# Crossbar transposes of queries and keys issued two steps ahead, in a fused ReLU-squared attention and channel-mixer kernel

## The chip, the cores and the metric

The kernel runs on one core of one Trainium2 chip. The metric is the device time of one execution in microseconds, lower is better; the profile gives the span from the first to the last instruction, which is 1.7 to 1.8 us shorter than the timed run. Every run is of one core, and a run counts as fast where it lies within 1.5% of the fastest of the same kernel in its series. "Landing" is the moment at which a transfer has arrived; the "granted clock" is the share of TensorE's full clock that the records show, and 0.5 is called half clock. In the profile lines PE is TensorE, PEld its weight loads, DVE the vector engine, ACT ScalarE, POOL GpSimd and SPq the queue of SyncE.

## The reference, cut to what matters

```python
# q, k, v: (8 batches, 12 heads, 448 tokens, 64), float32
scores = matmul(q, k.transpose(0, 1, 3, 2)) / sqrt(64)
attn   = maximum(scores, 0) ** 2 / 448
x      = heads side by side of matmul(attn, v)                      # (8, 448, 768)
u      = x + (maximum(x.T @ w_tok1, 0) @ w_tok2).T                  # token mixing, 448 -> 256 -> 448
out    = u + maximum(u @ w_ch1, 0) @ w_ch2                          # channel mixing, 768 -> 1536 -> 768
```

Scores need queries and keys with the head dimension on partitions, but they arrive with tokens on partitions. So every group of four heads needs one transpose of q and k. There are 24 groups, called steps 0 to 23 here.

## The kernel before

Steps 0 to 10 are transposed by TensorE, steps 11 to 23 by a DMA transpose (through the crossbar) on the SyncE queue, out of a staging buffer `qk_sb` into which the vector engine interleaves q and k. The parts that the change and the argument touch:

```python
    TDMA = 11
    def interleave(i):                      # vector engine, L192
        t = attn.tile([128, 2, QC, 2, D], BF16, name="qk_sb", bufs=1)
        qk_tiles[i] = t
        for w in range(2):
            nc.vector.tensor_copy(t[:, w].rearrange("n c g d -> n g c d"), raws.pop((i, "qk"[w])))

    def transposes_dma(i):                  # SyncE queue, L198
        sb = attn.tile([128, 2, QC, 128], BF16, tag="qkT", name="qkT_x")     # pool attn: bufs=2
        nc.sync.dma_start_transpose(out=sb..., in_=qk_tiles.pop(i)...)
        qkT[i] = sb
    # ... cut: scores (L217 on TensorE, L231 on ScalarE, squares L238 on the vector engine),
    # ... values (L250), x_back (L294: a DMA transpose of x), u_back (L413: of u), token and channel layers

    for i in range(DB + 1, ND + 2):         # one step; DB = 3, ND = 24
        # ... cut
        if i < ND:
            scores(i, 0); scores(i, 1)
        if 0 <= i - 1 < ND:
            values(i - 1, range(QC)); values_out(i - 1)
        if i < ND:
            scores(i, 2)
        # ... cut: filler matmuls of the channel layers while i - 1 < XDMA
        if 0 <= i - 1 < ND:
            x_back(i - 1)
        # ... cut
            while u_later and ...:
                u_back(u_later.pop(0))
        if TDMA <= i + 1 < ND:
            transposes_dma(i + 1)           # for the next step
        if i + PRE < ND:                    # PRE = 3
            if i - 1 >= XDMA:
                nc.gpsimd.tensor_copy(gate, x_tiles[i - 1][:1, 1, 3, 127:])   # wait until x has landed
            load_four(i + PRE)              # six loads of q, k, v on the GpSimd queue
        square()
        # ... cut: filler matmuls; scores 3 and 4; transposes(i + 1) on TensorE while i + 1 < TDMA
        square()
        # ... cut: filler matmuls, token layer 1 (L339, L355), scores 5 and 6
        if not slow:
            square()
            fill(0.1, least=1)
        if back:
            token2(i - 1)                   # L380 on TensorE, L390 on the vector engine
        # ... cut
        square()
        if TDMA <= i + 2 < ND:
            interleave(i + 2)
        fill(1 / 3 if slow else 0.16, least=1)
```

`fill` takes ready-made units of channel work from a queue: six L431 matmuls (evacuated by ScalarE) or twelve L470 matmuls (evacuated by the vector engine, L477). The program fixes the order of the matmuls; a change of the waits leaves that order as it is.

Of the kernel before, what the change touches and what calls it, by code (L numbers as in the profile page):

```python
# [10 lines left out]
BF16 = mybir.dt.bfloat16  # L11
# [5 lines left out]
def kernel(  # L17
# [13 lines left out]
    B, H, S, D = q.shape  # L31
# [5 lines left out]
    ND = B * H // 4  # L37
    DB = H // 4
    QC = S // 64
# [12 lines left out]
    attn = ctx.enter_context(tc.tile_pool(name="attn", bufs=2))  # L52
# [70 lines left out]
    qkT, at2, squares, accs = {}, {}, [], {}  # L123

    def transposes(i, place="acc", split=False):
        sb = attn.tile([128, 2, 2, S], BF16, name="qkT")
        if place == "att":
            both = ps_att.tile([128, 2, 1024], BF16, tag="att", name="qkT_ps")
            parts = [both[:, r] for r in range(2)]
        else:  # L130
            pool, tags = (ps_acc, ("acc0", "acc1")) if place == "acc" else (ps_mm, ("bank", "bank"))
            parts = [pool.tile([128, 1024], BF16, tag=tag, name="qkT_ps1") for tag in tags]
        for w in (1, 0) if i == 0 else (0, 1):
            src = raws.pop((i, "qk"[w]))
            for c in range(QC):
                at = w * S + c * 64
                for r in range(2):
                    h = slice(64 * r, 64 * (r + 1))
                    for g in range(2):
                        nc.tensor.matmul(  # L140
                            parts[r][64 * g : 64 * (g + 1), at : at + 64],
                            lhsT=src[h, g, c, :],
                            rhs=ident[h, h],
                            is_transpose=True,
                            start=True,
                            stop=True,
                            skip_group_check=True,
                        )
        qkT[i] = sb
        if place == "att":  # L150
            nc.vector.tensor_copy(sb.rearrange("n r w t -> n r (w t)"), both[:, :, : 2 * S])
            return
        for r in range(2):
            (nc.scalar.copy if split and r == 0 else nc.vector.tensor_copy)(
                sb[:, r].rearrange("n w t -> n (w t)"), parts[r][:, : 2 * S]
            )

    def transposes_first():

        sb = attn.tile([128, 2, 2, S], BF16, name="qkT")  # L160
        qkT[0] = sb
        keys = [ps_acc.tile([128, 1024], BF16, tag=f"acc{r}", name="kT_ps") for r in range(2)]
        queries = ps_att.tile([128, 2, 1024], BF16, tag="att", name="qT_ps")
        for w, dst in ((1, keys), (0, [queries[:, r] for r in range(2)])):
            for c in range(QC):
                for r in range(2):
                    h = slice(64 * r, 64 * (r + 1))
                    for g in range(2):
                        nc.tensor.matmul(
                            dst[r][64 * g : 64 * (g + 1), c * 64 : c * 64 + 64],  # L170
                            lhsT=raws[0, "qk"[w]][h, g, c, :],
                            rhs=ident[h, h],
                            is_transpose=True,
                            start=True,
                            stop=True,
                            skip_group_check=True,
                        )
            if w:
                nc.scalar.copy(sb[:, 0, 1], keys[0][:, :S])
                nc.vector.tensor_copy(sb[:, 1, 1], keys[1][:, :S])  # L180
            else:
                nc.vector.tensor_copy(sb[:, :, 0], queries[:, :, :S])

    TDMA = 11
    qk_tiles = {}

    def interleave(i):
# [4 lines that stand above are left out]
            nc.vector.tensor_copy(  # L192
                t[:, w].rearrange("n c g d -> n g c d"), raws.pop((i, "qk"[w]))
            )

    def transposes_dma(i):
        sb = attn.tile([128, 2, QC, 128], BF16, tag="qkT", name="qkT_x")
        nc.sync.dma_start_transpose(  # L198
            out=sb.rearrange("n w c t -> n (w c) t"),
            in_=qk_tiles.pop(i).rearrange("n w c g d -> n (w c g d)"),  # L200
        )
        qkT[i] = sb

    def qk_of(i, h, r):
        sb = qkT[i]
        if i < TDMA:
            return sb[h, r, 0, :], [sb[h, r, 1, c * 64 : (c + 1) * 64] for c in range(QC)]
        cols = slice(64 * r, 64 * (r + 1))
        return sb[h, 0, :, cols], [sb[h, 1, c, cols] for c in range(QC)]

    def scores(i, c, alone=False):
        ps = ps_att.tile([128, 2, 512], FP32, tag="att", name="sc_ps")
        for r in range(2):
            for g in range(2):
                h = slice(64 * g, 64 * (g + 1))
                queries, keys = qk_of(i, h, r)
                nc.tensor.matmul(  # L217
                    ps[64 * r : 64 * (r + 1), g, :S],
                    lhsT=keys[c],
                    rhs=queries,  # L220
                    start=True,
                    stop=True,
                    skip_group_check=True,
                )
        at = attn.tile([128, 2, S], BF16, name="at", bufs=12)
        if alone:
            nc.vector.tensor_scalar(
                out=at, in0=ps[:, :, :S], scalar1=0.0, scalar2=None, op0=ALU.max
            )
        else:  # L230
            nc.scalar.activation(at, ps[:, :, :S], AF.Relu)  # L231
        squares.append(at)
        at2[i, c] = at
# [184 lines left out]
    def hold_back(b, src):  # L418

        u_tiles[b] = mix.tile([128, NP, NT - NT // 2, 128], BF16, name="u_sb", bufs=3)  # L420
        for p in range(NP):
            nc.gpsimd.tensor_copy(u_tiles[b][:1, p, 0, :1], src)
# [206 lines left out]
    i = DB  # L629
# [31 lines left out]
    for i in range(DB + 1, ND + 2):  # L661
        slow = i <= 2 * DB
        back = i - 1 < ND
        if i == 2 * DB + 1:
            rate[0] = (EC * C1 + NT * C2) / DB
        if i < ND:
            scores(i, 0)
            scores(i, 1)
        if 0 <= i - 1 < ND:
            values(i - 1, range(QC))  # L670
            values_out(i - 1)
        if i < ND:
            scores(i, 2)
        if i - 1 < XDMA:
            fill(1 / 3, least=1)
        if 0 <= i - 1 < ND:
            x_back(i - 1)
        since[0] = 0.0
        if i > 2 * DB + 1:
            if i == 2 * DB + 2:  # L680
                hold_back(1, x_tiles[i - 1][:1, 0, 0, :1])
            while u_later and u_later[0] < max(i - 1 - (i == 2 * DB + 2), 0):
                u_back(u_later.pop(0))
        if TDMA <= i + 1 < ND:
            transposes_dma(i + 1)
        if i + PRE < ND:
            if i - 1 >= XDMA:
                nc.gpsimd.tensor_copy(gate, x_tiles[i - 1][:1, 1, 3, 127:])  # L688
            load_four(i + PRE)
        if i == 5:  # L690
            load_wc2(1, 2)
            load_wt1_last()
        square()
        if i - 1 >= XDMA:
            fill(0.37, least=1)
        if i < ND:
            scores(i, 3)
            scores(i, 4)
        if i + 1 < min(ND, TDMA):
            transposes(i + 1)  # L700
        square()
        if slow:
            token1(i - 1)
            fill(1 / 3, least=1)
        else:
            fill(0.37, least=1, upto=4400 if back else 0)
            if back:
                token1_main(i - 1)
        if i < ND:
            if not slow:  # L710
                token1_rest(i - 1)
            scores(i, 5)
            scores(i, 6)
        elif back:
            token1_rest(i - 1)
# [4 lines that stand above are left out]
            token2(i - 1)  # L720
            if (i - 1) % DB == DB - 1:
                channel_work((i - 1) // DB)
        if i == 2 * DB + 1:
            hold_back(0, uT_tiles[1][:1, 0, :1])
            for _ in range(DB):
                u_back(u_later.pop(0))
        square()
        if TDMA <= i + 2 < ND:
            interleave(i + 2)
        fill(1 / 3 if slow else 0.16, least=1)  # L730
    while queue:
        queue.pop(0)[1]()
# [30 lines left out]
```

## Time and profile before

| | before |
|---|---|
| time, median of the runs beside the changed kernel | 385.73 us (384.25 to 388.74, 4 runs; 387.2 of the first three was known to the prediction) |
| span of the profiled run | 385.1 us |
| TensorE busy, idle | 360.8 us, 24.3 us |
| TensorE waits for the crossbar transpose (L217 on qkT_x) | 15.4 us in 6 waits |
| granted TensorE clock, mean | 0.991 |

The page, the waits and a step are read line by line in the prediction below. It says that six loads are issued beside the transpose, but not what sets them off. That stands in the timeline of the kernel before, in the step that starts at 144.60 us:

```profile
151.44 0.18 POOL L688 COPY gate<-x_sb 1x1 bf16<-1x1 bf16 x1 [7.44 <-DMA x_sb<-xT]
...
151.95 1.19 POOL L83 DMA_DIRECT2D q_raw<-in_q_dram  x2 [0.34 <-issue]
```

Columns of the timeline: start, duration, engine, line, operation, tiles, then the idle time before it and what ended it. The loads wait behind a gate until x has landed; they start at 151.95 us, and the transpose of q and k is issued at 151.97 us (its line is in the prediction). The two set out together.

### The profile page before, as it was taken

Reading aid. Unit: us, or ns where it says so; the run is one execution under the profiler, and the core shown is the slowest. Engines: PE = TensorE matmul, PEld = TensorE weight load, DVE = VectorE, ACT = ScalarE, POOL = GpSimd, SP = SyncE. Lnnn points to the kernel's source line nnn. Section 1 sums busy time; section 2 is a strip of 40 time slices with the busy share of each in tenths; the row PEclk is TensorE's granted clock in tenths of the full one; section 3 lists DMA queues with packets and bytes.
Section 4 is the critical chain, followed back from the end, with each engine's and each line's share of the span. In section 5 each row is a group of like instructions: output and inputs, shape, how many; then the busy total and the mean of one; then the engine's idle time right before and its main releaser. Section 6 shows DMA issues by size and latency. Waiting matters only on the chain.

```text
span 385.1 us, 8830 instructions
## 1 busy us (share of the span) xinstructions
PE 360.8 (94%) x3649; PEld 193.2 (50%) x3649; DVE 208.4 (54%) x414; ACT 210.9 (55%) x313; POOL 99.0 (26%) x185
## 2 busy tenths in 40 slices
PE   8889999999999989899899999699949999999995
PEld 4444555556565544454455544355425555555564
DVE  2986788746567655656637655365523845321022
ACT  4987888764544577446664566534727437311400
POOL 9948346305030332131241232230300000000000
PEclk9999999999999999999999999989989999999999
DMA  8999999925998985896795987968755364234024
GB/s 154 123 203 171 194 195 159 142 36 92 186 113 171 234 156 88 143 174 147 121 138 119 204 137 135 118 81 202 115 69 97 78 142 97 54 44 107 0 51 115
DMA packets 93273, 49.19 MB, mean 128 GB/s; under 512 B 67185, under 2 KB 89777, under 8 KB 93233
## 3 DMA queue, kind: packets, MB, share of 16 engines
q0 software_dynamic: 24496, 21.49, 39.6%
q1 hardware_dynamic: 68352, 26.72, 34.6%
q8 instruction: 28, 0.46, 0.5%
q10 hardware_dynamic: 384, 0.43, 0.4%
q14 instruction: 13, 0.10, 0.1%
HBM read 43.42 MB, written 11.01 MB: 141 GB/s over the span
## 4 chain that ended last, share of the span: by engine, by line
PE 80%; DMA 12%; DVE 4%; ACT 1%; issue 1%; POOL 1%; ACTq 0%; DVEq 0%
PE m_ps L470 29%; PE m_ps L431 24%; DMA qkT_x<-qk_sb 11%; PE acc_ps L250 8%; PE sc_ps L217 8%; PE h_ps L380 3%; PE t_ps L339 2%; PE t_ps L321 1%; DVE uT_sb L390 1%; DVE at L238 1%; DMA k_raw<-in_k_dram 1%; PE warm_ps L566 1%; ACT at L231 1%; PE qkT_ps L140 1%; PE t_ps L355 1%
## 5 line engine op out<-in xcount | busy, mean ns | idle before, releaser
L231 ACT ACTIVATE at<-sc_ps 128x896 bf16<-128x896 f32 x167 | 144.9, 923 | 65.3 <-PE sc_ps L217 65.3
L238 DVE TENSOR_TENSOR at<-at 128x896 bf16<-128x896 bf16 x168 | 98.7, 620 | 65.8 <-ACT at L231 65.4
L431 PE MATMUL m_ps<-uT_sb,wc 128*128 128x448 bf16 x564 | 115.5, 353 | 0.2 <-DVE uT_sb L390 0.2
L470 PE MATMUL m_ps<-wc,r_sb 128*128 128x384 bf16 x660 | 114.0, 328 | 0.0
L470 PEld LDWEIGHTS <-r_sb 128*128 128x128 bf16 x660 | 63.0, 98 | 49.1 <-issue 9.1
L438 ACT ACTIVATE r_sb<-m_ps 128x448 bf16<-128x448 f32 x94 | 51.5, 548 | 53.0 <-PE m_ps L431 53.0
L431 PEld LDWEIGHTS <-wc 128*128 128x128 bf16 x564 | 52.3, 98 | 55.9 <-issue 11.1
L477 DVE TENSOR_TENSOR out_sb<-m_ps,u_sb 128x384 f32<-128x384 f32 x55 | 30.5, 554 | 45.3 <-PE m_ps L470 45.3
L250 PE MATMUL acc_ps<-at,v_raw 64*64 64x448 bf16 x672 | 40.5, 362 | 1.6 <-DVE x_sb L312 0.8
L217 PE MATMUL sc_ps<-qkT_x 64*64 64x448 bf16 x364 | 27.3, 363 | 15.4 <-DMA qkT_x<-qk_sb 15.4
L268 DVE TENSOR_SCALAR xT<-acc_ps 128x448 bf16<-128x448 f32 x45 | 26.1, 619 | 27.6 <-PE acc_ps L250 27.6
L688 POOL COPY gate<-x_sb 1x1 bf16<-1x1 bf16 x12 | 3.0, 248 | 131.3 <-DMA x_sb<-xT 131.3
L83 POOL DMA_DIRECT2D q_raw<-in_q_dram x48 | 28.9, 614 | 22.6 <-DMA wc<-in_moe_w_ch_dram 19.7
L390 DVE TENSOR_TENSOR uT_sb<-h_ps,xT 128x448 bf16<-128x448 f32 x48 | 27.7, 615 | 9.4 <-PE h_ps L380 9.3
L83 POOL DMA_DIRECT2D v_raw<-in_v_dram x48 | 29.6, 642 | 7.3 <-DMA wc<-in_moe_w_ch_dram 5.3
L250 PEld LDWEIGHTS <-v_raw 64*64 64x64 bf16 x672 | 21.1, 110 | 15.6 <-issue 5.0
L83 POOL DMA_DIRECT2D k_raw<-in_k_dram x46 | 28.2, 633 | 1.7 <-issue 1.7
L365 ACT ACTIVATE r_sb<-t_ps 128x256 bf16<-128x256 f32 x36 | 11.8, 381 | 30.1 <-PE t_ps L355 26.4
L217 PE MATMUL sc_ps<-qkT 64*64 64x448 bf16 x308 | 25.5, 360 | 0.9 <-ACT at L231 0.8
L380 PE MATMUL h_ps<-wt,r_sb 128*128 128x448 bf16 x96 | 22.3, 353 | 0.0
L217 PEld LDWEIGHTS <-qkT_x 64*64 64x64 bf16 x364 | 8.3, 107 | 25.8 <-DMA qkT_x<-qk_sb 18.3
L339 PE MATMUL t_ps<-x_sb,wt 128*128 128x256 bf16 x108 | 14.7, 273 | 0.0
(62 smaller groups left out, 161.4 us busy)
## 6 DMA issues: line engine op xcount, KB each, us to landing
out_dram<-out_sb SPq DMA_DIRECT2D x54, 192.0 KB, 3.3
q_raw<-in_q_dram POOLq DMA_DIRECT2D x48, 112.0 KB, 4.3
v_raw<-in_v_dram POOLq DMA_DIRECT2D x48, 112.0 KB, 6.8
k_raw<-in_k_dram POOLq DMA_DIRECT2D x46, 112.0 KB, 5.9
wc<-in_moe_w_ch_dram POOLq DMA_DIRECT2D x4, 1152.0 KB, 12.2
u_sb<-uT_sb SPq DMA_TRANSPOSE x48, 2.6
x_sb<-xT SPq DMA_TRANSPOSE x16, 3.3
k_first<-in_k_dram SPq DMA_DIRECT2D x1, 224.0 KB, 3.4
```

The costliest lines, as they stand in the source:

```text
L83: eng.dma_start(out=dst[64 * r : 64 * (r + 1)].rearrange("p g c d -> p g (c d)"), in_=src[b, h0 : h0 + 2].rearrange("g (p c) d -> p g (c d ...
L217: nc.tensor.matmul(ps[64 * r : 64 * (r + 1), g, :S], lhsT=keys[c], rhs=queries, start=True, stop=True, skip_group_check=True,)
L231: nc.scalar.activation(at, ps[:, :, :S], AF.Relu)
L238: nc.vector.tensor_tensor(out=at, in0=at, in1=at, op=ALU.mult)
L250: nc.tensor.matmul(ps[r][64 * g : 64 * (g + 1), :S], lhsT=v_raw[h, g, c, :], rhs=at[h, g, :], start=(c == 0), stop=(c == QC - 1), skip_gro ...
L268: nc.vector.tensor_scalar(out=xT[b % 2][:, 2 * d + r, :S], in0=ps[r][:, :S], scalar1=float(alpha2), scalar2=None, op0=ALU.mult,)
L380: nc.tensor.matmul(parts[r][:, :S], lhsT=r1[:, j, r * 128 : (r + 1) * 128], rhs=wt2[:, j, :], start=(j == 0), stop=(j == JC - 1),)
L390: nc.vector.tensor_tensor(out=uT_tiles[b // 2][:, 2 * d + r, off : off + S].rearrange("n (c p) -> n c p", c=QC), in0=parts[r][:, :S].rearr ...
L431: nc.tensor.matmul(ps[:, :S], lhsT=wc1[:, g, e * 128 : (e + 1) * 128], rhs=uT[:, g, off : off + S], start=(g == 0), stop=(g == CC - 1),)
L438: nc.scalar.activation(r2[:, e, off : off + S], ps[:, :S], AF.Relu)
L470: nc.tensor.matmul(ps[:, :HN], lhsT=r2[:, e, t * 128 : (t + 1) * 128], rhs=wc2[:, e, cols], start=(e == 0), stop=(e == EC - 1),)
L477: nc.vector.tensor_tensor(out=o[:, cols].rearrange("n (g d) -> n g d", d=128), in0=ps[:, :HN].rearrange("n (g d) -> n g d", d=128), in1=u_ ...
```

## The change

The intent is to take the crossbar transpose off TensorE's path by issuing it a step earlier. It needs its staged input earlier, so the interleaving copies move to the front of the step; a third transposed buffer is taken and one of twelve score buffers given up; and step 11 goes back to TensorE. The whole diff:

```diff
--- before.py
+++ after.py
@@ -123,7 +123,7 @@
     qkT, at2, squares, accs = {}, {}, [], {}
 
     def transposes(i, place="acc", split=False):
-        sb = attn.tile([128, 2, 2, S], BF16, name="qkT")
+        sb = attn.tile([128, 2, 2, S], BF16, name="qkT", bufs=3)
         if place == "att":
             both = ps_att.tile([128, 2, 1024], BF16, tag="att", name="qkT_ps")
             parts = [both[:, r] for r in range(2)]
@@ -157,7 +157,7 @@
 
     def transposes_first():
 
-        sb = attn.tile([128, 2, 2, S], BF16, name="qkT")
+        sb = attn.tile([128, 2, 2, S], BF16, name="qkT", bufs=3)
         qkT[0] = sb
         keys = [ps_acc.tile([128, 1024], BF16, tag=f"acc{r}", name="kT_ps") for r in range(2)]
         queries = ps_att.tile([128, 2, 1024], BF16, tag="att", name="qT_ps")
@@ -181,7 +181,7 @@
             else:
                 nc.vector.tensor_copy(sb[:, :, 0], queries[:, :, :S])
 
-    TDMA = 11
+    TDMA = 12
     qk_tiles = {}
 
     def interleave(i):
@@ -194,7 +194,7 @@
             )
 
     def transposes_dma(i):
-        sb = attn.tile([128, 2, QC, 128], BF16, tag="qkT", name="qkT_x")
+        sb = attn.tile([128, 2, QC, 128], BF16, tag="qkT", name="qkT_x", bufs=3)
         nc.sync.dma_start_transpose(
             out=sb.rearrange("n w c t -> n (w c) t"),
             in_=qk_tiles.pop(i).rearrange("n w c g d -> n (w c g d)"),
@@ -222,7 +222,7 @@
                     stop=True,
                     skip_group_check=True,
                 )
-        at = attn.tile([128, 2, S], BF16, name="at", bufs=12)
+        at = attn.tile([128, 2, S], BF16, name="at", bufs=11)
         if alone:
             nc.vector.tensor_scalar(
                 out=at, in0=ps[:, :, :S], scalar1=0.0, scalar2=None, op0=ALU.max
@@ -671,6 +671,8 @@
             values_out(i - 1)
         if i < ND:
             scores(i, 2)
+        if TDMA <= i + 2 < ND:
+            interleave(i + 2)
         if i - 1 < XDMA:
             fill(1 / 3, least=1)
         if 0 <= i - 1 < ND:
@@ -681,8 +683,8 @@
                 hold_back(1, x_tiles[i - 1][:1, 0, 0, :1])
             while u_later and u_later[0] < max(i - 1 - (i == 2 * DB + 2), 0):
                 u_back(u_later.pop(0))
-        if TDMA <= i + 1 < ND:
-            transposes_dma(i + 1)
+        if TDMA <= i + 2 < ND:
+            transposes_dma(i + 2)
         if i + PRE < ND:
             if i - 1 >= XDMA:
                 nc.gpsimd.tensor_copy(gate, x_tiles[i - 1][:1, 1, 3, 127:])
@@ -725,8 +727,6 @@
             for _ in range(DB):
                 u_back(u_later.pop(0))
         square()
-        if TDMA <= i + 2 < ND:
-            interleave(i + 2)
         fill(1 / 3 if slow else 0.16, least=1)
     while queue:
         queue.pop(0)[1]()
```

## The prediction

> **What bounds the kernel now.** I read the page's busy line and chain first, then the table of waits, then the timeline of single steps.
>
> ```profile
> PE 360.8 (94%) x3649; PEld 193.2 (50%) x3649; DVE 208.4 (54%) x414; ACT 210.9 (55%) x313; POOL 99.0 (26%) x185
> ...
> PE 80%; DMA 12%; DVE 4%; ACT 1%; issue 1%; POOL 1%; ACTq 0%; DVEq 0%
> PE m_ps L470 29%; PE m_ps L431 24%; DMA qkT_x<-qk_sb 11%; PE acc_ps L250 8%; PE sc_ps L217 8%; PE h_ps L380 3%; PE t_ps L339 2%; PE t_ps L321 1%; DVE uT_sb L390 1%; DVE at L238 1%; DMA k_raw<-in_k_dram 1%; PE warm_ps L566 1%; ACT at L231 1%; PE qkT_ps L140 1%; PE t_ps L355 1%
> ```
>
> TensorE sets the end: 94% busy, 80% of the chain. The one foreign piece of weight is the crossbar transpose of queries and keys (qkT_x), 11%, about 42 us. But the chain follows a released wait back to the transfer's issue, and TensorE was working through most of that time. What it lost is in the table of waits (us in total, times, longest):
>
> ```profile
> PEld L217 <- DMA qkT_x<-qk_sb: 18.3, 7, 6.3
> ...
> PE sc_ps L217 <- DMA qkT_x<-qk_sb: 15.4, 6, 5.8
> ...
> DVE qk_sb L192 <- DMA qkT_x<-qk_sb: 8.4, 2, 5.3
> DVE qk_sb L192 <- DMA k_raw<-in_k_dram: 4.1, 5, 1.2
> ```
>
> So 15.4 us in six waits is the prize; of the 24 us in which TensorE is idle at all (385.1 less 360.8), that is most. The six waits, read one by one before the first score matmul of a step, are 1.37, 1.44, 1.73, 1.42, 3.60 and 5.81 us. The timeline of one step shows why:
>
> ```profile
> 148.01 1.23 SPq L294 DMA_TRANSPOSE x_sb<-xT  x1
> 149.29 2.58 SPq L413 DMA_TRANSPOSE u_sb<-uT_sb  x2
> ...
> 151.97 1.59 SPq L198 DMA_TRANSPOSE qkT_x<-qk_sb  x1
> ...
> 157.77 0.57 PE L217 MATMUL sc_ps<-qkT_x 64*64 64x448 bf16 x8 [1.44 <-DMA qkT_x<-qk_sb]
> 157.85 0.39 DVE L192 COPY qk_sb<-q_raw 128x896 bf16<-128x896 bf16 x1 [0.92 <-DMA k_raw<-in_k_dram]
> ```
>
> The step starts at 144.60. The transpose for the next step stands third in the SyncE queue and is issued 7.4 us into it; it lands at 157.73. TensorE's own work in the step is done at 156.33 and it waits 1.44 us. The six waits stand at the ends of exactly the six steps whose TensorE work is only 11.7 to 12.9 us; steps of 14.6 us and more hide the transfer. The vector copy in the last line is charged to a key load, but those keys came a step earlier; it can start only when the transpose has read the single staging buffer qk_sb, so it too waits for this transfer.
>
> A long wait costs a second time:
>
> ```profile
> 273.98 10.16 DMA qkT_x<-qk_sb
> 284.19 0.96 PE sc_ps L217 x8
> 285.15 2.33 PE acc_ps L250 x27
> ...
> 301.73 1.32 PE acc_ps L250 x28
> ```
>
> After the 5.81 us wait, eight score matmuls take 0.96 us in place of 0.57 (0.57 stands in the other steps) and 27 value matmuls 2.33 us where 28 take 1.32. The clock records hold a stretch of 3.4 us at 0.5 there and another after the 3.60 us wait, where values take 1.99 and 24 output matmuls 4.79 in place of 4.01. Together 0.39 + 1.01 + 0.67 + 0.78 = 2.9 us.
>
> **What the Trainium skill says.** "TensorE: Matmul & The Clock Gate", Part 1: an idle window of about 3.4 us drops the array to half clock until about 3.4 us of work have passed. The trace agrees: both halved stretches are 3.41 us long and only the two waits above 3.4 us have one. "Trainium Kernel Development and Optimization", Key Constraints: DMAs from the SyncE, ScalarE and GpSimd queues share the same 16 DMA engines and interleave. The trace agrees: the transpose lands 4.6 and 5.5 us after issue in the last two steps, where no inputs are loaded, and 5.3 to 10.2 us where six loads are issued beside it. "Perfetto Trace Analysis", Tensor Engine Instruction: the vector engine is strictly first in, first out, so a copy that waits for data holds up all vector work behind it; the trace shows it, with vector idle up to 5.3 us ahead of L192.
>
> **The change, part by part.** I call step i the turn of the main loop that computes the scores of i.
>
> The transpose used in step i+2 is now issued in step i, at the same place of the SyncE queue, some 7.4 us in. Its deadline is a whole step later: 4 to 5 us of room (11.7 - 7.4) become 16 or more. The worst landing on record is 10.16 us. All six waits go: -15.4 us. The two halved stretches go with them: -2.9 us.
>
> Step 11 is transposed on TensorE once more. The same work in the step before shows its price:
>
> ```profile
> 106.26 0.39 PE L140 MATMUL qkT_ps<-ident,q_raw 64*64 64x64 bf16 x28
> 106.47 0.43 PE L140 MATMUL qkT_ps<-ident,k_raw 64*64 64x64 bf16 x28
> 106.84 4.07 PE L470 MATMUL m_ps<-wc,r_sb 128*128 128x384 bf16 x24
> ```
>
> 56 transposes take 106.84 - 106.26 = 0.6 us of TensorE, and two vector copies of 0.61 us which hide as they do there: +0.6 us. One of 13 crossbar transposes goes; it had no wait, so 0.
>
> The interleaving copies (2 x 0.39 us of vector time) move from a step's end to right behind the evacuation of the values, some 3.4 us into the step. They now need q and k landed by then: loads issued in the step before. With the landings of the trace and the steps shortened by their waits, k lands at +2.7 to +3.4 us in most short steps, so just in time, and at about +5.0 in one (after the step at 266.70); the staging buffer is free at +1.4 in most and about +5.8 in that one. That one vector stall of 2.4 us falls into a step whose next work is first-layer channel matmuls, evacuated by ScalarE, so it hides. In the second-layer steps the copies push the evacuation of an output bank by 0.8 us; the margin in the trace is about 1.2 us. I put down +0.5.
>
> The waits also hid smaller ones. The value matmuls take the accumulators that L390 still reads; in the later step at 328.97, which has no transpose wait, this costs 0.27 us. In the step starting at 144.60, L390 ends at 156.93 while value matmuls could start at 156.7. I take 0.2 us in each of six: +1.2. The x transpose (x_sb) lands only 0.5 us before its first matmul in short steps; where two short steps follow one another, the loads of the first now overlap it by about 1 us: +0.5.
>
> Three qkT buffers: the new transpose needs the buffer of step i-1, already free. Only once, where the order of taking buffers jumps (12 is taken before 11), 14 gets the buffer of 12 and is issued behind the last scores of that step, about 1.2 us later than otherwise; harmless. Eleven score buffers in place of twelve: scores c of a step then wait for values c-4 of the step before, which already stand ahead of them in TensorE's order: 0.
>
> Sum: -15.4 - 2.9 + 0.6 + 0.5 + 1.2 + 0.5 = -15.5 us. On the median of 387.2 that makes 371.7 us.
>
> **The rivals.** First, the wait moves to the vector engine: keys are not landed when the moved copies stand at the head of its queue, squares and evacuations queue behind them, and TensorE waits for banks. For it: margins of 0 to 0.7 us computed above. Against it: vector work is only 54% busy and late squares are needed only a step later. If every second-layer step lost 1 to 2 us, five such steps give back some 8 us: about 379.
>
> Second, the DMA engines become the bound: in the six short steps their share is 0.75 to 0.98 with the waits in, and taking 1.4 to 5.8 us out packs the same traffic closer, so that x transposes and loads come late. For it: transposes slowed to 8.3 and 10.2 us in the two densest steps. Against it: the long steps between leave slack (shares of 0.74 and 0.81), and the bytes do not grow. Half the gain lost would make about 378; all of it, 387.
>
> Third, the transfer is hidden anyway and the 11% is an artefact of the chain: refused by the six waits, which are idle TensorE.
>
> **Range and chances.** The saving has a hard core of 15.4 us plus the clock; 2% needs 7.7 us, so half of it may be lost. The runs of the kernel before spread over 4.5 us, and I allow for losses to the two rivals on the upper side: 367 to 378. Faster by over 2%: 0.90; within 2%: 0.09; slower: 0.01.
>
> **What would show each step.** Right: no wait of L217 for qkT_x of weight, span near 370; no 0.5 in the clock records after the start; 12 transposes on L198 issued more than a step before use; 56 more L140 matmuls in one block of 0.6 us; new waits of L250 on L390 of 0.1 to 0.3 us. Wrong: L192 with long idle for k_raw or qkT_x and TensorE waiting behind L477 (first rival); L339 waiting for x_sb, or landings of 8 us and more in all steps (second). A wait of L217 that stays would mean that the transposes are issued later than I think, by a buffer or a queue slot.

## The result

| | before | after |
|---|---|---|
| time, median | 385.73 us (384.25 to 388.74, 4 runs) | 371.31 us (371.05 to 371.69, 4 runs) |
| ratio of fast runs | | 0.9618, 95% interval 0.9548 to 0.9687 |
| span of the profiled run | 385.1 us | 369.8 us |
| granted clock | 0.991 | 0.998 |
| transposes on L198: number, issue to landing (min, median, max) | 13; 4.6, 5.9, 10.2 us | 12; 4.0, 6.1, 7.9 us |

A ratio is the mean time of one kernel's fast runs over the mean of the other's fast runs of the same rounds, so it is not quite the ratio of the medians. The predicted time was 371.7 us.

The page of the changed kernel, busy line and shares of the chain:

```profile
PE 359.9 (97%) x3705; PEld 193.5 (52%) x3705; DVE 207.3 (56%) x414; ACT 210.5 (57%) x313; POOL 98.6 (27%) x185
...
PE 86%; DVE 5%; DMA 4%; POOL 2%; issue 1%; ACT 1%; DVEq 0%; POOLq 0%; ACTq 0%
```

TensorE is idle for 9.9 us (369.8 less 359.9) where it was 24.3. The 56 more matmuls are there (3705 against 3649). The waits of the changed kernel from 100 to 330 us (total, times, longest):

```profile
PEld L217 <- DMA qkT_x<-qk_sb: 0.4, 1, 0.4
...
DVE qk_sb L192 <- DMA qkT_x<-qk_sb: 0.3, 1, 0.3
PE m_ps L431 <- DVE out_sb L477: 0.2, 1, 0.2
```

No score matmul waits for the crossbar any more; only one weight load sits idle for 0.4 us. The vector engine waits once for the staging buffer, and one output evacuation is late by 0.2 us. The clock records of the changed kernel hold no stretch of 0.5 between the first 7 us and the last 2. A short step in the timeline of the changed kernel, the same step as in the prediction's third extract:

```profile
143.32 1.15 DVE L390 TENSOR_TENSOR uT_sb<-h_ps,xT 128x448 bf16<-128x448 f32 x2
...
143.81 0.57 PE L217 MATMUL sc_ps<-qkT_x 64*64 64x448 bf16 x8
...
144.21 1.83 PE L250 MATMUL acc_ps<-at,v_raw 64*64 64x448 bf16 x28
...
151.36 1.52 SPq L198 DMA_TRANSPOSE qkT_x<-qk_sb  x1
...
155.81 0.57 PE L217 MATMUL sc_ps<-qkT_x 64*64 64x448 bf16 x8
```

The transpose is still issued 7.5 us into the step and lands at 157.26 us (issue plus its landing time of 5.91 us), after the next step has begun at 155.81 us. That costs nothing, because it is now meant for the step after that one. And there is a new, small cost: the 28 value matmuls take 1.83 us where 1.49 to 1.50 us was usual.

The block of TensorE transposes for step 11 in the changed kernel:

```profile
121.52 0.39 PE L140 MATMUL qkT_ps<-ident,q_raw 64*64 64x64 bf16 x28
...
122.10 4.08 PE L470 MATMUL m_ps<-wc,r_sb 128*128 128x384 bf16 x24
```

From its start to the next matmul it takes 122.10 - 121.52 = 0.58 us.

### The profile page after: what moved, and what is told of

Same layout as the page of the kernel before. It is cut to its first block, busy times and chain, and to the rows that moved or that the text cites. A ratio compares the mean times of both kernels' runs of the same rounds, so it can differ in the third digit from the quotient of the medians.

```text
span 369.8 us, 8951 instructions
## 1 busy us (share of the span) xinstructions
PE 359.9 (97%) x3705; PEld 193.5 (52%) x3705; DVE 207.3 (56%) x414; ACT 210.5 (57%) x313; POOL 98.6 (27%) x185
## 4 chain that ended last, share of the span: by engine, by line
PE 86%; DVE 5%; DMA 4%; POOL 2%; issue 1%; ACT 1%; DVEq 0%; POOLq 0%; ACTq 0%
PE m_ps L431 28%; PE m_ps L470 28%; PE acc_ps L250 9%; PE sc_ps L217 8%; PE h_ps L380 4%; PE t_ps L339 3%; DVE at L238 1%; DMA x_sb<-xT 1%; PE t_ps L321 1%; DVE uT_sb L390 1%; DMA q_raw<-in_q_dram 1%; PE t_ps L355 1%; DMA k_raw<-in_k_dram 1%; PE qkT_ps L140 1%; POOL q_raw L83 1%
## 5 line engine op out<-in xcount | busy, mean ns | idle before, releaser
L431 PE MATMUL m_ps<-uT_sb,wc 128*128 128x448 bf16 x564 | 115.7, 353 | 0.4 <-DVE out_sb L477 0.2
L431 PEld LDWEIGHTS <-wc 128*128 128x128 bf16 x564 | 52.3, 98 | 56.3 <-issue 11.6
L477 DVE TENSOR_TENSOR out_sb<-m_ps,u_sb 128x384 f32<-128x384 f32 x55 | 30.5, 555 | 48.7 <-PE m_ps L470 45.5
L390 DVE TENSOR_TENSOR uT_sb<-h_ps,xT 128x448 bf16<-128x448 f32 x48 | 27.7, 616 | 9.4 <-PE h_ps L380 9.3
L217 PE MATMUL sc_ps<-qkT 64*64 64x448 bf16 x336 | 27.5, 360 | 1.0 <-ACT at L231 0.8
L217 PE MATMUL sc_ps<-qkT_x 64*64 64x448 bf16 x336 | 25.7, 356 | 0.0
L217 PEld LDWEIGHTS <-qkT 64*64 64x64 bf16 x336 | 9.2, 105 | 12.9 <-issue 10.5
L339 PE MATMUL t_ps<-x_sb,wt 128*128 128x256 bf16 x108 | 14.7, 273 | 0.1
## 6 DMA issues: line engine op xcount, KB each, us to landing
wc<-in_moe_w_ch_dram POOLq DMA_DIRECT2D x4, 1152.0 KB, 11.7
```

What stands on the lines that cost most here:

```text
L217: nc.tensor.matmul(ps[64 * r : 64 * (r + 1), g, :S], lhsT=keys[c], rhs=queries, start=True, stop=True, skip_group_check=True,)
L390: nc.vector.tensor_tensor(out=uT_tiles[b // 2][:, 2 * d + r, off : off + S].rearrange("n (c p) -> n c p", c=QC), in0=parts[r][:, :S].rearr ...
L431: nc.tensor.matmul(ps[:, :S], lhsT=wc1[:, g, e * 128 : (e + 1) * 128], rhs=uT[:, g, off : off + S], start=(g == 0), stop=(g == CC - 1),)
L477: nc.vector.tensor_tensor(out=o[:, cols].rearrange("n (g d) -> n g d", d=128), in0=ps[:, :HN].rearrange("n (g d) -> n g d", d=128), in1=u_ ...
```

## The experiments

My theory: what counts is when the transpose is issued against when it is needed; buffers and copies only make that possible. The main rivals: the gain is the third buffer; the DMA engines are the bound and only a long lead copes with them; the moved copies turn the vector engine into a new wait. I do not compare medians of different series more closely than a microsecond or two: the kernel before itself spreads from 381.1 to 391.7 us over the three series. Two pieces of the change were not run by themselves in the kernel before: step 11 on TensorE, and the earlier copies.

### e1: the buffers alone

```diff
-        sb = attn.tile([128, 2, 2, S], BF16, name="qkT")            # both places, and L197
+        sb = attn.tile([128, 2, 2, S], BF16, name="qkT", bufs=3)
-        at = attn.tile([128, 2, S], BF16, name="at", bufs=12)
+        at = attn.tile([128, 2, S], BF16, name="at", bufs=11)
```

> The kernel before with three transposed buffers and eleven score buffers, and nothing moved. Theory (the time of issue is what counts): unchanged, ratio to the kernel before 0.99 to 1.01, and the L217 waits for qkT_x still sum to 12 to 18 us, because the transpose stands behind the x and u transposes in the SyncE queue and not behind a buffer. Rival (the transpose waits for its buffer, as the queue's waits of L198 for score matmuls suggest, and the third buffer is the gain): ratio near 0.96, waits gone.

Measured: 383.59 us (382.35 to 384.07), ratio 0.9935, interval 0.9867 to 1.0002. Its waits:

```profile
PE sc_ps L217 <- DMA qkT_x<-qk_sb: 11.7, 5, 5.8
```

The sum, 11.7 us, is just under the range that I gave, and five waits stand where six did, but the waits are there and the time is the same within 2%. The third buffer alone is not the gain.

### e2: the same lead, front of the queue

```diff
+        if TDMA <= i + 1 < ND:
+            transposes_dma(i + 1)
         if 0 <= i - 1 < ND:
             values(i - 1, range(QC)); values_out(i - 1)
         ...
-        if TDMA <= i + 1 < ND:              # behind x_back and u_back
-            transposes_dma(i + 1)
```

> The kernel before, one step ahead and with two buffers as it was, only the transpose for the next step put in front of the x and u transposes of its step. Theory (lead time alone): issued about 7 us earlier, landing by +8 us of a step that lasts 11.7 us or more, so no L217 wait for qkT_x: 15.4 us of waits and 2.9 us of half clock gone. Price to be seen: the x transpose now shares the crossbar with it and its matmuls have only 0.5 us of margin, so L339 waits of 0 to 1.5 us in short steps. Time 367 to 376 us, ratio 0.955 to 0.975. Rival (two steps of lead are needed because the DMA engines are the bound): most waits stay, ratio above 0.98.

Measured: 376.67 us (372.52 to 377.33), ratio 0.9729, interval 0.9649 to 0.9809, verdict unclear, for the interval crosses 0.98. In its profiled run all waits of L217 for qkT_x are gone, in a kernel that looks one step ahead with two buffers. So two steps of lead are not needed. The foreseen price is there too, in its timeline:

```profile
174.65 1.65 SPq L198 DMA_TRANSPOSE qkT_x<-qk_sb  x1
...
176.40 1.85 SPq L294 DMA_TRANSPOSE x_sb<-xT  x1
...
180.24 0.83 PE L339 MATMUL t_ps<-x_sb,wt 128*128 128x256 bf16 x6 [0.93 <-DMA x_sb<-xT]
```

The x transpose queues behind it and token matmuls wait, 1.9 us in four waits in the profiled run. That run was the fastest of four, 372.5 us; what costs the other three some 4 us more, no trace shows.

### e3: the same lead, later in the step

```diff
-        if TDMA <= i + 1 < ND:              # behind x_back and u_back
-            transposes_dma(i + 1)
         ...
             scores(i, 5)
             scores(i, 6)
+            if TDMA <= i + 1 < ND:
+                transposes_dma(i + 1)
```

> The kernel before with the transpose issued later in the same step, behind the last score matmuls (about 8.6 us into the step in place of 7.4). Theory: each of the six waits grows by about 1.2 us, so +7 us, and more of them pass 3.4 us and are followed by a half clock stretch at 1.5 us each: 393 to 398 us, ratio 1.018 to 1.035. Rival (the transfer is hidden or the waits have another cause): ratio 1.00.

Measured: 411.17 us in the one run that counts as fast, which is also the profiled one (the other three 417.8 to 419.2); no interval. The direction is right, the size is two to three times what I expected. The waits of L217 sum to 32.8 us in ten places, 17.4 us more than before, and the mean clock is 0.965. One of them, in its timeline:

```profile
242.67 4.77 SPq L198 DMA_TRANSPOSE qkT_x<-qk_sb  x1
...
254.77 0.96 PE L217 MATMUL sc_ps<-qkT_x 64*64 64x448 bf16 x8 [7.36 <-DMA qkT_x<-qk_sb]
```

The edit did not do what I had assumed, a delay of 1.2 us in every step. The call stands behind the last scores in the program, but in its queue it follows whatever was put there before it. SyncE, in the steps that start at 150.25 and 163.02 us:

```profile
157.63 1.54 SPq L198 DMA_TRANSPOSE qkT_x<-qk_sb  x1
...
170.42 5.09 SPq L489 DMA_DIRECT2D out_dram<-out_sb  x4
175.61 3.95 SPq L198 DMA_TRANSPOSE qkT_x<-qk_sb  x1
```

The first is issued 7.38 us into its step, no later than before. The second stands behind four output stores and is issued 12.59 us in. And I had kept the landing fixed, but issued behind output stores and beside the loads, the transpose at 242.67 us took 12.06 us to land. So e3 shows that a worse place in the queue costs a lot, not what a delay of 1.2 us costs; and the rule "wait = issue + landing - work of the step" needs an issue and a landing that belong to the place in the queue.

### e4: two steps ahead with two buffers

```diff
 (the changed kernel, with qkT at bufs=2 and at at bufs=12)
-        if TDMA <= i + 2 < ND:              # behind x_back and u_back
-            transposes_dma(i + 2)
         ...
             scores(i, 5)
             scores(i, 6)
+            if TDMA <= i + 2 < ND:
+                transposes_dma(i + 2)
```

> Two steps ahead with the early interleaving copies, but only two transposed buffers and twelve score buffers: the transpose for i+2 is issued behind the last scores of step i, whose buffer it takes, about 8.6 us into step i. Theory: the deadline is still a step later, 15 us of room against a worst landing of 10 us, so as fast as the changed kernel: ratio to the kernel before 0.955 to 0.970, no L217 waits for qkT_x of weight; vector copies may stall up to 2 us on the staging buffer without harm. Rival (the third buffer is needed): ratio above 0.98.

Measured: 385.0 us (381.69 to 387.74), ratio 0.9938, interval 0.9855 to 1.0022. My expectation failed. Not one score matmul waits for qkT_x, and nothing is gained. Its waits show where the gain went:

```profile
DVE qk_sb L192 <- DMA qkT_x<-qk_sb: 23.0, 7, 4.9
...
PE m_ps L470 <- DVE out_sb L477: 8.0, 3, 2.8
```

and its timeline shows one of the three:

```profile
162.78 0.39 DVE L192 COPY qk_sb<-q_raw 128x896 bf16<-128x896 bf16 x1 [3.43 <-DMA qkT_x<-qk_sb]
...
165.60 2.72 PE L470 MATMUL m_ps<-wc,r_sb 128*128 128x384 bf16 x8 [2.84 <-DVE out_sb L477]
```

This is the prediction's first rival come true: the next interleaving copy must wait until the late transpose has read the single staging buffer. The copy stands early in the vector engine's order, so squares and output evacuations queue behind it, and TensorE waits for a bank of PSUM. Issued behind the last scores, its transposes take 9.1 us at the median to land, where the changed kernel has 6.1. The harm that I had called none is 8.0 us here, and half clock after one of the waits.

### e9: the same with a second staging buffer

```diff
 (e4)
-        t = attn.tile([128, 2, QC, 2, D], BF16, name="qk_sb", bufs=1)
+        t = attn.tile([128, 2, QC, 2, D], BF16, name="qk_sb", bufs=2)
-        at = attn.tile([128, 2, S], BF16, name="at", bufs=12)
+        at = attn.tile([128, 2, S], BF16, name="at", bufs=11)
```

> The two-buffer kernel of two steps ahead (which gained almost nothing) with a second staging buffer qk_sb and eleven score buffers, so with as much memory as the changed kernel. Theory (what stopped it was the vector engine stalled on the single staging buffer, with output evacuations behind it): stalls of L192 on qkT_x gone, TensorE waits for L477 (8.0 us) gone, about 371 us, ratio 0.955 to 0.97. Rival (the late issue beside the output stores fills the DMA engines): ratio stays above 0.98.

Measured: 375.66 us (373.28 to 377.4), ratio 0.9725, interval 0.967 to 0.978. The ratio lies just above the range of the theory and below that of the rival.

```profile
DVE qk_sb L192 <- DMA k_raw<-in_k_dram: 7.7, 6, 2.5
...
PE m_ps L470 <- DVE out_sb L477: 1.7, 1, 1.7
```

The stalls on the staging buffer are gone and the L477 waits fall from 8.0 to 1.7 us, so the cause found in e4 is confirmed for most of the loss. The rest is not settled: the vector engine now waits for keys (7.7 us in six waits), and five of its twelve transposes still take 9.4 to 11.4 us to land, as the rival would have it; what that costs was not isolated.

### e5, e6, e7: the small terms of the sum

The yardstick of this series is the changed kernel once more:

> The changed kernel once more, as the yardstick of this series on the same chip: about 371 us, ratio to the kernel before 0.955 to 0.97.

Measured: 371.16 us (371.12 to 372.33), ratio to the kernel before 0.9685, interval 0.9649 to 0.9722. Six of the eleven runs of the kernel before in this series count as slow, and the recorded verdict against it is unclear for all four kernels of the series. So e5 to e7 are compared with this yardstick, whose runs are all fast, as theirs are.

e5 gives step 11 back to the crossbar:

```diff
 (the changed kernel)
-    TDMA = 12
+    TDMA = 11
```

> The changed kernel with step 11 transposed by the crossbar again, as in the kernel before. Theory: the block of 56 matmuls costs 0.6 us and nothing else, so 0.6 us faster than the changed kernel of this series (0.2 to 1.0). Rival: the transposes on TensorE were needed because the DMA engines are full in the steps before (share 1.05 there), and the crossbar transposes of steps 9 and 10 push the x transposes or the output stores: 1 to 3 us slower, with L339 or L470 waits near 105 to 135 us.

Measured: 374.51 us (371.52 to 376.86), ratio 0.976, interval 0.9699 to 0.9822; 3.3 us slower than the changed kernel by medians. The rival was right in that it is slower and where, but TensorE waits for the vector engine and not for x. Its timeline:

```profile
123.24 0.39 DVE L192 COPY qk_sb<-q_raw 128x896 bf16<-128x896 bf16 x1 [3.21 <-DMA qkT_x<-qk_sb]
...
126.06 2.11 PE L470 MATMUL m_ps<-wc,r_sb 128*128 128x384 bf16 x12 [2.68 <-DVE out_sb L477]
```

The extra transpose, issued at 112.53 us, takes 10.22 us to land among the u transposes and loads of those steps; the next interleaving copy waits for its staging buffer, and TensorE waits 2.68 us behind the vector engine. The block on TensorE costs 0.58 us and avoids this. That is what step 11 on TensorE buys in this kernel; the prediction had booked it as a cost only.

e6 moves one square per step behind L390 in the changed kernel:

```diff
         if not slow:
-            square()
+            square(keep=1)
             fill(0.1, least=1)
```

> The changed kernel with one score square per step moved behind the two L390 additions in the vector engine's order, so that the accumulators come free about 0.6 us earlier. Theory: in the short steps the value matmuls take 1.83 us in place of 1.50 because they wait for L390, 0.33 us in six steps: 2.0 us faster than the changed kernel of this series (1.2 to 2.4), value matmuls back at 1.50 us everywhere. Rival: the 0.33 us is something else in the start of the step, or the later square holds up the last value matmuls by as much: no gain.

Measured: 369.17 us (368.61 to 369.64), ratio to the kernel before 0.9623, interval 0.9588 to 0.9657; 2.0 us faster than the changed kernel by medians, as expected. Its timeline, at the place of the changed kernel's extract above:

```profile
142.61 1.15 DVE L390 TENSOR_TENSOR uT_sb<-h_ps,xT 128x448 bf16<-128x448 f32 x2
...
144.30 1.49 PE L250 MATMUL acc_ps<-at,v_raw 64*64 64x448 bf16 x28
```

L390 starts at 142.61 us in place of 143.32, and all value groups of the main steps are back at 1.49 us; in the changed kernel six of them stood at 1.83 that had not before.

e7 has both edits:

> Both of the last two edits on the changed kernel. If both theories hold, 2.6 us faster than the changed kernel of this series: about 368.7 us.

Measured: 372.25 us (370.34 to 374.91), ratio 0.9719, interval 0.967 to 0.9769. That is 1.1 us slower than the yardstick, where the two edits measured 3.3 us slower and 2.0 us faster: they add up, but not to the 368.7 us expected. Its trace keeps a wait of 2.3 us for L477 at 125.75 us, and the value matmuls are not held up.

### e10: the second staging buffer there

```diff
 (e7)
-        t = attn.tile([128, 2, QC, 2, D], BF16, name="qk_sb", bufs=1)
+        t = attn.tile([128, 2, QC, 2, D], BF16, name="qk_sb", bufs=2)
-        at = attn.tile([128, 2, S], BF16, name="at", bufs=11)
+        at = attn.tile([128, 2, S], BF16, name="at", bufs=9)
```

> The changed kernel with step 11 by crossbar and the last square later (e7), and a second staging buffer paid for by two score buffers (nine). Theory: the 2.3 us wait for L477 near 125 us, which came from the vector engine stalled on the staging buffer behind a 10 us transpose, is gone: 2 to 3 us faster than e7, about 0.6 us faster than e6, some 368.5 us, ratio 0.95 to 0.965. Rival (the DMA engines themselves are full there): L339 then waits for x_sb and it stays at 371 us or more.

Measured: 368.55 us (367.73 to 372.98), ratio 0.9559, interval 0.9501 to 0.9617. The 2.3 us wait for L477 is gone; L339 now waits 1.3 us for x_sb at 126.28 us, as the rival had it, but the time is where the theory put it. Whether it beats e6 the intervals do not say, for they overlap.

### e8: matmuls on zeros inside the two long waits

```diff
 (the kernel before, at the end of a step)
+        if i in (18, 20):
+            idle_ps = ps_mm.tile([128, 512], FP32, tag="bank", name="idle_ps")
+            for m in range(12):
+                nc.tensor.matmul(idle_ps, lhsT=warm[:, :128], rhs=warm, start=True, stop=True)
```

> The kernel before with twelve matmuls on zeros (about 2.6 us) in front of the waits at the ends of steps 18 and 20, the two that were over 3.4 us long; nothing reads their result. Theory (such waits cost a second time through the half clock): the dummies lie inside the waits, no 0.5 stretch after the start is left in the clock records, and the time falls by up to 2.9 us: ratio to the kernel before 0.985 to 1.000. Rival (the clock drop has another cause, or costs nothing): the 0.5 stretches stay, ratio 1.00 to 1.01.

Measured: 382.55 us (379.96 to 385.44), ratio 0.9901, interval 0.9836 to 0.9965. The output is still correct (nothing reads the dummies). In size this fits the theory, but it does not isolate the clock. In its profiled run the transposes of steps 18 to 20 also landed sooner (5.1 to 6.3 us, where the kernel before had 7.5 to 10.2), so that the waits fell from 15.4 to 7.4 us, by more than the 5.2 us of dummies that took their place. And one stretch of half clock stayed, in its busy time by windows (length, then busy time and count per engine, the clock, DMA share and GB/s at the end):

```profile
186.00:188.30 2.30, 0.17 (x1) 0.00 (x0) 0.76 (x2) 0.54 (x1) 0.00 (x0) 1.00 1.15 144
188.30:191.70 3.40, 3.25 (x36) 1.68 (x40) 0.70 (x2) 1.73 (x2) 0.00 (x0) 0.50 0.38 60
```

It follows a wait of only 2.3 us. The cost of half clock is therefore read from durations in the trace (0.96 against 0.57 us), not from this experiment.

### e11: ahead of the u transposes, nothing else

```diff
 (the kernel before)
         if 0 <= i - 1 < ND:
             x_back(i - 1)
         since[0] = 0.0
+        if TDMA <= i + 1 < ND:
+            transposes_dma(i + 1)
         if i > 2 * DB + 1:
             ...                             # u_back
-        if TDMA <= i + 1 < ND:
-            transposes_dma(i + 1)
```

> The kernel before, one step ahead, two buffers, only the transpose put ahead of the u transposes in the SyncE queue (behind the x transpose as before): issued 2.6 us earlier. Theory (each wait is issue plus landing minus the step's work): the waits of 1.4 to 1.7 us vanish, 3.6 and 5.8 shrink to about 1.0 and 3.2, so 4 us in place of 15.4 and no half clock: 370 to 376 us, ratio 0.962 to 0.978. Rival (the landing is set by the loads beside it, whenever it is issued): waits shrink by less than half, ratio above 0.98.

Measured: 370.0 us (369.81 to 370.16), ratio 0.958, interval 0.9532 to 0.9628. It does better than I expected: no wait of L217 for qkT_x is left at all. Its timeline, SyncE and GpSimd queues, in the step that starts at 143.12 us:

```profile
146.69 1.23 SPq L294 DMA_TRANSPOSE x_sb<-xT  x1
148.02 1.59 SPq L198 DMA_TRANSPOSE qkT_x<-qk_sb  x1
149.66 3.11 SPq L413 DMA_TRANSPOSE u_sb<-uT_sb  x2
...
150.66 1.19 POOL L83 DMA_DIRECT2D q_raw<-in_q_dram  x2 [0.34 <-issue]
```

and the summary of its transposes on this tile, beside the 4.6, 5.9 and 10.2 us of the kernel before:

```profile
DMA to landing us min/median/max: 4.0/4.2/5.9
```

Issued 4.9 us into the step, the transpose is 2.6 us ahead of the loads, which still wait for x. It lands at 152.12 us, 4.1 us after issue, when the next step is 3.0 us away. In the kernel before it set out with the loads and took 5.76 us at the same place. So moving one call pays twice: 2.5 us earlier in its step, and 1.7 us shorter by the medians of landing. Whether it is the loads or the u transposes that it gets away from, no run isolates. The last two transposes, which have no loads beside them, point to the loads: they land in 5.53 and 4.60 us before and in 4.12 and 5.64 us here, no gain on average. The u transposes now land later, 4.6 us at the median in place of 2.6, and nothing waits for them after 100 us. With two transposed buffers, twelve score buffers and step 11 on the crossbar, it reaches the time of the changed kernel or a little better. It still has the 1.83 us value groups; with e6's edit on top it might reach 368 us, but that was not run.

## Why the prediction was right

The time (371.7 predicted, 371.31 measured) and the mechanism came out as put down. That the time agrees to 0.4 us is in part luck: the saving of the medians is 385.73 - 371.31 = 14.4 us and not 15.5, and the base of 387.2 us was 1.5 us too high. Point by point:

- **The six waits, -15.4 us.** Right. None is left. e1 shows that the buffer alone does not remove them, e2 and e11 that an earlier place in the queue does.
- **Half clock, -2.9 us.** The stretches are gone, as forecast. The 2.9 us is a reading of durations in one run; how much it is on average no experiment isolates. The reason "only the waits above 3.4 us have one" did not hold in other runs: stretches of 0.5 go with waits of 2.29 us (e8), 2.80 us (e3) and 2.84 us (e4).
- **Step 11 on TensorE, +0.6 us.** The block is 0.58 us. That the crossbar transpose which goes was worth nothing ("it had no wait, so 0") was right for the kernel before and wrong for a kernel of two steps ahead: in e5, keeping it costs 3.3 us.
- **The moved copies, +0.5 us.** One L431 matmul waits 0.2 us for L477. The 2.4 us vector stall that I expected in one step did not come, in a trace whose longest landing is 7.9 us. The mechanism is real, as e4 and e5 show, at 8.0 and 2.7 us; the changed kernel stays clear of it with little to spare.
- **The accumulators, +1.2 us.** Right in place, low in size: 0.34 us in six groups is 2.0 us where 0.2 us in each was put down, and e6 wins it back.
- **x_sb, +0.5 us.** Nothing in the short steps. It did come in e2, at 1.9 us.
- **Buffers, 0.** Right in the sum. The one transpose said to be issued 1.2 us late, for 14, was issued 7.55 us into its step (151.36 less 143.81), before that step's last scores at 152.20: the buffers were not taken in the order that I worked out. It had no effect.
- **Two readings of the prediction were wrong.** The landing of 10.2 us is not in one of the two densest steps: its step has a DMA share of 0.82, below 0.93 and 0.83 in others. And half of the 15.5 us lost would make 379.4 us, not 378. Neither is a term of the sum.

The measured terms are -15.4 - 2.9 + 0.6 + 0.2 + 2.0 = -15.5 us against a span shorter by 385.1 - 369.8 = 15.3 us. So two small errors, on the copies and x on one side and on the accumulators on the other, cancelled out: that is luck too.

What the prediction did not see is that the lead of a second step was not the only cure. It saw that the transfer stood third in its queue and met six loads, and asked only how much room it had, not whether it could stand elsewhere. In e11 it goes ahead of two u transposes that nothing there waits for, and sets out before the loads.

## What to carry to other kernels

When a consumer waits for a DMA, look first at what stands ahead of the transfer in its own queue and what is set off at the same moment; reordering one call can be worth as much as another buffer and a step of lead (370.0 us against 371.2 here, in different series). A deeper prefetch can move the wait upstream, as in e4, to whoever refills the staging buffer, so check which engine queues behind that refill. And where a wait disappears, look for the small waits that it covered: moving one vector instruction per step was worth 2.0 us in the changed kernel; in the kernel before, the short steps show no such loss to win back (1.49 to 1.50 us, half clock aside).

## What the Trainium skill lacked or had wrong

- "TensorE: Matmul & The Clock Gate", the table in "Why this matters for your kernels", advises no idle gaps above about 3 us. Here 3.41 us at 0.5 go with a wait of 2.29 us (e8, before 188.45 us), of 2.80 us (e3) and of 2.84 us (e4), and none with waits of 2.50 and 2.71 us (e4). The page does say in Part 1 that the window runs freely; the runs show that a gap shorter than the window can be enough.
- "Advanced Engine Details and Errata", X-Bar Transpose (TRN2), gives 350 to 400 GB/s as the expected rate of a crossbar transpose. Here one of 128 x 14 x 128 elements of 2 bytes, 459 KB, lands 4.1 us after an issue that is 2.6 us ahead of the loads (e11), about 112 GB/s with issue counted in. The runs do not separate a start-up cost from the rate.
- The pages say that queues share the DMA engines and interleave; none says what a transpose loses to loads issued beside it. The runs show a median landing of 4.2 us ahead of them (e11), 5.9 us beside them (the kernel before), and up to 12.1 us behind an output store and beside them (e3).
